# Softmax sums in another accumulator bank, a regrouped plan and new instruction orders in a one-core two-layer decode kernel

## The chip, the cores and the metric

The kernel runs on one core of a Trainium2 chip. A core has a matrix engine (TensorE, PE in the profile), a vector engine (VectorE, DVE), a scalar engine (ScalarE, ACT), a general engine (GpSimd, POOL) and one that here only issues transfers (SyncE, SP). Each engine runs its own list of instructions in the order in which they are written; engines wait for one another, and for transfers, by semaphores. Matrix products are accumulated in eight PSUM banks. The metric is the device time in microseconds (us) of one launch; smaller is better.

## The reference

One decode step for four tokens (one position each), width D = 448, through attention and a gated FFN, twice with the same weights and the same caches:

```python
x = A_x                                          # [4, 1, 448] bf16
x = x + attn(layernorm(x), k_cache, v_cache, wq, wo)
x = x + ffn(layernorm(x), w_gate, w_up, w_down)   # (silu(x@wg) * (x@wu)) @ wd, inner width 1792
x = x + attn(layernorm(x), k_cache, v_cache, wq, wo)
x = x + ffn(layernorm(x), w_gate, w_up, w_down)
```

`attn` has 16 query heads of 256, two to each of 8 key/value heads, and looks at the last 2048 of the 8192 cached positions: scores = q·k / 16, softmax, times v, then the output projection `wo`. Each token has keys and values of its own. "Layer 0" and "layer 1" are the two passes; since a token attends only to its cache, one token's layer 1 can run while another is still in layer 0.

## The kernel before, in words

**Store and loads.** One token's K for one key/value head is 1 MB, V another. They are loaded in halves of 512 KB into `half`, a store of 38 units of that size: 31 are free from the start, the last 7 hold `wq` first and are used for K and V only after the last q projection. Of each token's eight heads in layer 0, the six processed last are kept in the store until layer 1 has used them ("kept pairs"); heads 0 and 1 are loaded again. That makes 80 K units and 80 V units; K comes in at L976/L978 (a load of both halves at once where the order says `a+b`) and V at L992, all issued by SP in the order `SEQ_SP` and into the units listed in `SLOTS`. A load into a used unit waits for the instruction that last read it: the scores for K, P times V for V.

**Batches and plan.** `PLAN` is a list of steps; a step has one or more batches, and a batch is two pairs written as token, layer, head: `212+213` is token 2, layer 1, heads 2 and 3. There are 32 batches. The function `group` (from L957) builds one:
- VectorE transposes each newly loaded K unit (L982); GpSimd or VectorE spreads the query `qe` (L1023).
- TensorE makes the scores (L1016) in bank S0 or S1, the two taking turns by batch. VectorE takes the maximum (L1031), TensorE spreads it (L1036, L1039), VectorE negates it (L1045), and ScalarE takes the exponential into `praw` (L1049).
- TensorE turns the probabilities into one of three Y banks (L1060), ScalarE copies them to `pT` (L1068), TensorE sums them (`total`, L1076) and VectorE reduces the sums to `rs` (L1081).
- TensorE multiplies by V into columns 256 to 511 of that Y bank (L1090, four groups of matmuls). GpSimd takes the reciprocal of `rs` (L1103), ScalarE and VectorE copy the product out as `oh` (L1105, L1107), TensorE flips it (L1113), and VectorE scales it into `oT` (L1123).

`out_proj` then multiplies `oT` with `wo_sb` as a column (L1135) or as rows (L1143) into bank A.

**A token's way between its layers.** When all eight heads of a token are through, `rows` (L883 to L897) and `residual` (L903, L875) add up x. `norm` (L589 to L625) takes mean and variance, `ffn` makes gate and up (L801), the activation, and down (L853, the last product of the FFN), a second `norm` follows, and `qproj` (L683 to L722) makes the queries of layer 1 for that token. Banks Z and Z2 serve all of this. Only then can the token's layer 1 begin: its first batch is the scores of kept pairs, which then give their units back.

**What sets the order.** Everything is a node of `Graph`, with the keys it reads and writes and its `bank`. Two instructions on different engines that name the same bank wait for each other in program order, whatever columns they touch. The order on each engine is written out by hand as numbers of nodes: `SEQ_PE`, `SEQ_DVE`, `SEQ_ACT`, `SEQ_POOL`, `SEQ_SP`. A `w` in `SEQ_PE` is a filler (L1253), a matmul of zeros into bank A that keeps TensorE busy; `HELD` says after which filler the readers of bank A may come. `schedule` puts the waits in place.

Of the kernel before, what the change touches and what calls it, by code (L numbers as in the profile page):

```python
# [86 lines left out]
).split()  # L87
SEQ_DVE = (
# [280 lines left out]
def build(nc, A_x, A_k_cache, A_v_cache, A_wq, A_wo, B_x, B_w_gate, B_w_up, B_w_down, out):  # L369
    s0 = A_k_cache.shape[2] - WIN  # L370
    g = Graph()
# [958 lines left out]
```

## Time and profile before

| | |
|---|---|
| median of 3 runs | 283.61 us (282.2 to 283.75) |
| the profiled execution, in all | 285.95 us |
| its span, first to last instruction | 284.2 us |
| mean granted TensorE clock in it | 0.976 |
| TensorE busy, 4437 matmuls | 75% of the span |
| VectorE busy | 61% |
| GpSimd busy | 27% |
| ScalarE busy | 17% |
| moved by DMA | 96.70 MB, 340 GB/s on average |
| of that through the data queues | 96.06 MB, of which 80 MiB are K and V |

The page gives busy shares over the whole span, 40 slices of it, the chain of waits that ended last and the costliest groups of instructions. A group's row reads: line, engine, operation, output and input, shape, count, then busy time and mean ns of one, then the engine's idle time just before such instructions and what ended most of it. A row in the chain, or in a timeline, reads: start in us, length in us, engine, operands, line. A row of the windows reads: stretch, its length, the busy us of PE, weight loads, DVE, ACT and POOL with their counts, the mean granted clock, the DMA share and GB/s. The slices of the DMA's share, in tenths, show where transfers run dry:

```profile
PE   0000077799787888898998598899987889898997
PEclk9999999999779999999999999999998999999998
DMA  6999999999998999998798999937999999499200
```

The first seventh of the span is the loading of weights and first keys, the last tenth has no transfers left.

### The profile page before, as it was taken

Reading aid. Unit: us, or ns where it says so; the run is one execution under the profiler, and the core shown is the slowest. Engines: PE = TensorE matmul, PEld = TensorE weight load, DVE = VectorE, ACT = ScalarE, POOL = GpSimd, SP = SyncE. Lnnn points to the kernel's source line nnn. Section 1 sums busy time; section 2 is a strip of 40 time slices with the busy share of each in tenths; the row PEclk is TensorE's granted clock in tenths of the full one; section 3 lists DMA queues with packets and bytes.
Section 4 is the critical chain, followed back from the end, with each engine's and each line's share of the span. In section 5 each row is a group of like instructions: output and inputs, shape, how many; then the busy total and the mean of one; then the engine's idle time right before and its main releaser. Section 6 shows DMA issues by size and latency. Waiting matters only on the chain.

```text
span 284.2 us, 9987 instructions
## 1 busy us (share of the span) xinstructions
PE 213.9 (75%) x4437; PEld 124.3 (44%) x4437; DVE 174.7 (61%) x522; ACT 47.7 (17%) x115; POOL 76.3 (27%) x195
## 2 busy tenths in 40 slices
PE   0000077799787888898998598899987889898997
PEld 0000032355553533545654253475533545545584
DVE  7716255546434798656568686474997566548751
ACT  0000000232010221221112032201221132023410
POOL 1000027242203322231152035123231331243371
PEclk9999999999779999999999999999998999999998
DMA  6999999999998999998798999937999999499200
GB/s 238 405 413 409 408 413 406 405 404 396 380 386 309 329 407 412 407 409 340 243 343 310 413 411 409 404 148 300 381 379 413 409 408 371 164 338 406 78 5 3
DMA packets 28330, 96.70 MB, mean 340 GB/s; under 512 B 2811, under 2 KB 6911, under 8 KB 27519
## 3 DMA queue, kind: packets, MB, share of 16 engines
q1 hardware_dynamic: 28279, 96.06, 87.4%
q8 instruction: 35, 0.57, 0.8%
q14 instruction: 8, 0.07, 0.1%
q10 hardware_dynamic: 8, 0.00, 0.0%
HBM read 96.05 MB, written 0.00 MB: 338 GB/s over the span
## 4 chain that ended last, share of the span: by engine, by line
PE 46%; DMA 30%; SPq 9%; DVE 6%; issue 3%; ACT 3%; POOL 2%; ACTq 0%
DMA half<-in_A_k_cache_dram 13%; PE A L1253 12%; PE S L1016 8%; DMA wd_sb<-in_B_w_down_dram 6%; DMA half<-in_A_v_cache_dram 6%; DMA wo_sb<-in_A_x_dram 6%; PE Y L1090 5%; SPq L976 4%; PE Z L801 4%; SPq L992 3%; PE Z L683 3%; PE Z L853 3%; DVE half L982 3%; PE A L1143 2%; PE Y L1060 2%
## 5 line engine op out<-in xcount | busy, mean ns | idle before, releaser
L982 DVE STREAM_TRANSPOSE half<-half 128x1024 uint32<-128x1024 uint32 x80 | 97.4, 1230 | 23.9 <-DMA half<-in_A_k_cache_dram 23.8
L1253 PE MATMUL A<-identb,small 128*128 128x512 bf16 x236 | 72.6, 403 | 1.1 <-ACT wide L883 0.8
L1103 POOL TENSOR_TENSOR small<-small 128x4 f32<-128x4 f32 x32 | 32.5, 1018 | 52.3 <-DVE small L1081 49.0
L1090 PE MATMUL Y<-half,pT 128*8 128x256 bf16 x1024 | 38.8, 273 | 3.2 <-DVE small L1081 1.7
L1016 PE MATMUL S<-half,qe 128*8 128x256 bf16 (+1 forms) x1120 | 36.0, 272 | 6.6 <-DVE half L982 4.0
L1016 PEld LDWEIGHTS S<-half,qe 128*8 128x8 bf16 x1120 | 24.6, 85 | 17.1 <-DVE half L982 5.9
L921 PE MATMUL Z<-identb,wo_sb 4*128 4x4 bf16 x4 | 0.3, 166 | 37.6 <-DMA wo_sb<-in_A_x_dram 37.6
L1023 POOL TENSOR_TENSOR qe<-qc,small 128x64 bf16<-128x64 bf16 x56 | 15.4, 295 | 47.6 <-PE S L1016 36.9
L1253 PEld LDWEIGHTS A<-identb,small 128*128 128x128 bf16 x236 | 20.0, 105 | 16.7 <-issue 8.6
L1090 PEld LDWEIGHTS Y<-half,pT 128*8 128x8 bf16 x1024 | 21.1, 85 | 12.0 <-DVE small L1081 4.2
L615 POOL TENSOR_SCALAR st<-st 128x1 f32<-128x1 f32 x16 | 4.5, 283 | 80.4 <-DVE st L609 80.3
L1031 DVE TENSOR_REDUCE small<-S 104x1 bf16<-104x256 f32 x32 | 13.3, 416 | 18.7 <-PE S L1016 18.7
L1105 ACT ACTIVATE oh<-Y 128x256 bf16<-128x256 f32 x32 | 12.2, 383 | 55.2 <-PE Y L1090 46.7
L1107 DVE SCALAR_TENSOR_TENSOR oh<-oh,small,Y 128x256 bf16<-128x256 bf16 x32 | 14.9, 467 | 4.0 <-ACT oh L1105 3.8
L921 PEld LDWEIGHTS Z<-identb,wo_sb 4*128 4x128 bf16 x4 | 0.2, 102 | 37.6 <-DMA wo_sb<-in_A_x_dram 37.6
L1068 ACT ACTIVATE pT<-Y 128x192 bf16<-128x192 f32 x32 | 10.5, 329 | 23.3 <-PE Y L1060 16.7
L1143 PE MATMUL A<-wo_sb,oT 128*4 128x448 bf16 x200 | 14.0, 352 | 0.4 <-DVE oT L1123 0.4
L683 PE MATMUL Z<-half,small 128*5 128x512 bf16 x160 | 11.8, 379 | 2.9 <-DVE small L592 1.5
L1049 ACT ACTIVATE praw<-S,small,st 104x256 bf16<-104x256 f32 x16 | 9.0, 563 | 26.8 <-DVE small L1045 24.9
L1049 ACT ACTIVATE praw<-S,small 104x256 bf16<-104x256 f32 x16 | 7.6, 472 | 32.0 <-DVE small L1045 31.2
L1060 PE MATMUL Y<-selt,praw 104*64 104x48 bf16 x256 | 9.9, 194 | 3.6 <-ACT praw L1049 3.6
L1123 DVE TENSOR_TENSOR oT<-Y,small 128x4 bf16<-128x4 f32 x64 | 8.4, 156 | 5.8 <-PE Y L1113 4.5
(135 smaller groups left out, 244.2 us busy)
## 6 DMA issues: line engine op xcount, KB each, us to landing
half<-in_A_v_cache_dram SPq DMA_DIRECT2D x80, 512.0 KB, 12.7
half<-in_A_k_cache_dram SPq DMA_DIRECT2D x74, 512.0 KB, 8.6
wo_sb<-in_A_wo_dram SPq DMA_DIRECT2D x8, 448.0 KB, 13.2
half<-in_A_wq_dram SPq DMA_DIRECT2D x3, 1024.0 KB, 14.3
half<-in_A_k_cache_dram SPq DMA_DIRECT2D x3, 1024.0 KB, 15.3
wd_sb<-in_B_w_down_dram SPq DMA_DIRECT2D x1, 1568.0 KB, 17.2
wg_sb<-in_B_w_gate_dram SPq DMA_DIRECT2D x1, 1344.0 KB, 10.7
wu_sb<-in_B_w_up_dram SPq DMA_DIRECT2D x1, 1344.0 KB, 15.2
```

The source lines that it names most:

```text
L683: last = e.matmul(zb[32 * j:32 * j + B + 1, 0:512], lhsT=lhsT, rhs=wq_sb[:, c:c + 512], start=(cc == 0), stop=(cc == 3), skip_group_check= ...
L982: return e.transpose(a, a)
L1016: last = e.matmul(Sb[s_][qd:qd + 8, c0:c0 + rhs.free_size()], lhsT=qe[q_][:, P, ce, :, :].rearrange("p a n -> p (a n)"), rhs=rhs, start=(c ...
L1023: g.op(*((DVE, 0.13) if layer and fresh.get(t, gi) == gi else (POOL, 0.25)), pos - SLEAD - 1, lambda e, P=P, t=t, kvh=kvh: e.tensor_tensor ...
L1031: g.op(DVE, (0.23, 0.36)[n - 1], pos, lambda e: e.tensor_reduce(pmax[s_][0:R, :], Sb[s_][0:R, 0:N], AX.X, ALU.max), r=(f"s{s_}",), w=(f"pm ...
L1049: return e.activation(praw[0:R, 0:128 * n].rearrange("p (g r l) -> p g r l", g=2 * n, l=2), Sb[s_][0:R, 0:128 * n].rearrange("p (l g r) -> ...
L1060: last = e.matmul(Yb[p_][64 * h:64 * h + 64, c0:c0 + (48 if n == 2 else 32)], lhsT=praw[0:R, 64 * gg:64 * gg + 64], rhs=w, start=(gg == 0) ...
L1090: last = e.matmul(Yb[p_][32 * gg:32 * gg + M, 256:512], lhsT=pT[pt][:, gg, 2 * a + hv, 4 * P:4 * P + M] if n == 2 else p1[:, gg % 2, 2 * a ...
L1103: g.op(POOL, 0.69, pos, lambda e: e.tensor_tensor(ri[p_][:, 0:2 * n], rs[p_][:, 0:2 * n], expo[:, 1:1 + 2 * n], op=ALU.pow), r=(f"rs{p_}", ...
L1107: g.op(DVE, 0.43, pos, lambda e: e.scalar_tensor_tensor(out=oh[:, :], in0=oh[:, :], scalar=lomask[:, 0:1], in1=Yb[p_][:, 256:512], op0=ALU ...
L1143: last = e.matmul(Ab[32 * k:32 * k + B, 0:D], lhsT=oT[oi][:, k % 2, k // 2, :], rhs=wo_sb[:, 4 * kvh + k, :], start=False, stop=False, ski ...
L1253: return e.matmul(Ab[:, 0:512], lhsT=zero[:, 0:1].broadcast_to([128, 128]), rhs=identb[:, :].unsqueeze(1).broadcast_to([128, 4, 128]), sta ...
```

## The change

Three things, in one diff.

**1. The sums.** The sum over the probabilities is written to columns 288 and up of the batch's score bank, where it went to columns 192 and up of its Y bank. The reduction reads it there. The first of the two matmuls now starts its accumulation, since the bank isn't zeroed ahead. The node names the S bank for both, so P times V no longer waits for the reduction by way of the Y bank, and the scores of the batch that takes the same S bank next do.

```diff
-            sums = Yb[p_][:, 192:192 + 32 * n].rearrange("p (k P n) -> p k P n", k=16, n=2)
+            sums = Sb[s_][:, 288:288 + 32 * n].rearrange("p (k P n) -> p k P n", k=16, n=2)
 
             def total(e):
...
-                                    start=False, stop=False, skip_group_check=True)
+                                    start=(P == 0), stop=False, skip_group_check=True)
                 return last
-            g.op(PE, 0.06 * n, pos, total, r=(f"pT{pt}", "onesb"), w=(f"ysum{p_}",), bank=(f"Y{p_}",))
+            g.op(PE, 0.06 * n, pos, total, r=(f"pT{pt}", "onesb"), w=(f"m{s_}",), bank=(f"S{s_}",))
             g.op(DVE, 0.2, pos, lambda e: e.tensor_reduce(
                 rs[p_][:, 0:2 * n].rearrange("p (P n) -> p P n", n=2), sums.rearrange("p k P n -> p P n k"), AX.X, ALU.add),
-                r=(f"ysum{p_}",), w=(f"rs{p_}",), bank=(f"Y{p_}",))
+                r=(f"m{s_}",), w=(f"rs{p_}",), bank=(f"S{s_}",))
```

**2. The plan.** Two steps of token 1's kept pairs become one, and token 2's kept pairs are put together otherwise:

```diff
-    "106+107", "200+201", "010+011", "115+113", "116+112", "114+117", "202+203", "204+205", "206+207", "300+301",
-    "212+213 214+215", "216+217 302+303", "306+305", "304+307", "110+111", "210+211 316+313", "314+315",
+    "106+107", "200+201", "010+011", "115+113", "116+112 114+117", "202+203", "204+205", "206+207", "300+301",
+    "212+213 217+215", "216+214 302+303", "306+305", "304+307", "110+111", "210+211 316+313", "314+315",
     "312+317", "310+311",
```

**3. The orders.** `SEQ_PE`, `SEQ_DVE`, `SEQ_ACT`, `SEQ_POOL`, `SEQ_SP`, `SLOTS` and `HELD` are new lists throughout. Apart from the fillers (232 for 236), the instructions on each compute engine are the same in number and kind. SP has 175 issues for 176, since four K loads are paired for three. Compared instruction by instruction, with batches named by token, layer and head:

- VectorE, beginning of token 1's stage: maximum and negation of 100+101 come ahead of the last steps of token 0's FFN (L835 to L846).
- VectorE, end of token 1's and token 2's last batches: the transposition of a K unit of 010 comes ahead of the scaling of 107's output, that of one of 301 ahead of 207's; before, behind them. At the maximum of 316+313, two transpositions of 311 stand ahead; before, one of 310.
- TensorE: scores 100+101 lie inside token 0's gate and up; sum and first P times V of 100+101 lie ahead of token 0's q projection. P times V of 010+011 and of 200+201 lie ahead of the scores of 112 and 113; before, the first behind both. P times V of 300+301 lies between the parts of token 2's q projection, and token 2's down projection stands behind scores 300+301, two fillers and the spread of their maximum. P times V of 313 and 315 lies ahead of the scores of 317.
- TensorE's fillers up to the down projection of tokens 0, 1, 2 and 3: 53, 119, 171 and 217, for 48, 115, 162 and 221 before.
- SP: the last V load of token 2's layer 0 is at place 117 for 119, with 66.69 MB in front of it for 67.21. Five loads, for six, use the space of `wq`. Each load is directed to another unit.

```diff
 SLOTS = (
-    "0 1 2 3 4 5 6 7 8 9 10 11 12 13 14 15 16 17 18 19 20 21 22 23 24 25 26 27 28 29 30 14 15 18 19 26 4 28 8 9 10 18 "
...
+    "0 1 2 3 4 5 6 7 8 9 10 11 12 13 14 15 16 17 18 19 20 21 22 23 24 25 26 27 28 29 30 9 10 15 23 24 18 30 17 11 21 "
...
```

More of the change, by code (lines that the diff above doesn't have):

```diff
@@ L125 @@
 SEQ_SP = (
[7 rows of a table removed]
[7 rows of a table added]
 ).split()
 SLOTS = (
[4 rows of a table removed]
[4 rows of a table added]
 ).split()
 HELD = (
-    "0 44 44 44 102 102 108 108 140 142 142 142 151 151 158 158 208 208 215 215 227 228 228 228 228 228 228 228 228 "
-    "228 228 228"
+    "0 44 44 46 106 106 116 116 136 142 145 145 159 159 166 166 213 213 213 213 218 220 224 224 224 224 224 224 224 "
+    "224 224 224"
 ).split()
```

128 rows, old and new, of tables (SEQ_ACT, SEQ_DVE, SEQ_PE, SEQ_POOL) are left out of this document.

## The prediction

> **What bounds the kernel now.** I read the page first, for the busy shares:
>
> ```profile
> PE 213.9 (75%) x4437; PEld 124.3 (44%) x4437; DVE 174.7 (61%) x522; ACT 47.7 (17%) x115; POOL 76.3 (27%) x195
> ```
>
> No engine is full. Then the windows, cut at the ends of the four tokens' first layers (columns: stretch, length, busy us of PE, PEld, DVE, ACT, POOL, then the granted PE clock, the DMA share and GB/s):
>
> ```profile
> 84.40:127.00 42.60, 37.27 (x687) 19.38 (x685) 29.51 (x68) 8.62 (x22) 12.75 (x29) 1.00 0.98 379
> 127.00:149.00 22.00, 20.47 (x484) 13.19 (x483) 13.47 (x47) 3.35 (x8) 6.46 (x18) 1.00 0.85 312
> 149.00:184.00 35.00, 27.47 (x562) 14.34 (x561) 24.01 (x59) 7.93 (x20) 10.47 (x23) 1.00 1.00 389
> 184.00:203.00 19.00, 18.02 (x460) 12.09 (x459) 12.13 (x41) 2.44 (x6) 5.53 (x17) 1.00 0.69 266
> 203.00:238.00 35.00, 29.93 (x538) 15.31 (x537) 24.89 (x54) 8.58 (x21) 9.86 (x21) 0.95 1.02 399
> 238.00:258.00 20.00, 18.62 (x443) 11.73 (x444) 12.53 (x42) 2.04 (x5) 5.47 (x16) 1.00 0.79 283
> 258.00:284.20 26.20, 22.27 (x595) 15.97 (x587) 14.75 (x68) 7.03 (x17) 9.89 (x24) 0.93 0.26 100
> ```
>
> Loads and a chain take turns. In the long stretches the transfers are full (0.98 to 1.02). In the stretches where a token passes from attention through its FFN to its next q, they run dry: 22.0 x 0.15 = 3.3 us, 19.0 x 0.31 = 5.9 us, 20.0 x 0.21 = 4.2 us are lost. There all 31 units of the K/V store are taken, and a load is issued only when the scores or P times V of a batch give a unit back. SyncE's own timeline shows the largest hole:
>
> ```profile
> 174.43 18.47 SPq L992 DMA_DIRECT2D half<-in_A_v_cache_dram  x3
> 192.94 2.02 SPq L976 DMA_DIRECT2D half<-in_A_k_cache_dram  x2
> ```
>
> Three issues take 18.47 us: the second of them waits for the scores of 300+301, which end at 192.06. So the path is: a token's last loads land, chain to the next scores, units given back, loads, the next token. After the last loads a chain of 26 us remains. The chain of waits has the stage ends on which I count (start, us, what):
>
> ```profile
> 83.39 1.05 PE Z L853 x42
> ...
> 92.95 2.09 PE S L1016 x56
> ...
> 138.98 1.50 PE Z L853 x56
> ...
> 182.43 0.17 PE Y L1076 x2
> ...
> 182.62 0.23 DVE small L1081
> ...
> 182.90 1.05 PE Y L1090 x32
> ...
> 192.06 1.50 PE Z L853 x56
> ...
> 248.24 1.50 PE Z L853 x56
> ```
>
> L853 is the FFN's down projection: tokens 0 to 3 are through it at 84.44, 140.48, 193.56 and 249.74. The span is 284.2.
>
> **The change part by part.** *Sums into the scores' bank.* Nothing is added or removed: the same two matmuls, the same reduction, at the prices of these rows:
>
> ```profile
> L982 DVE STREAM_TRANSPOSE half<-half 128x1024 uint32<-128x1024 uint32 x80 | 97.4, 1230 | 23.9 <-DMA half<-in_A_k_cache_dram 23.8
> ...
> L1031 DVE TENSOR_REDUCE small<-S 104x1 bf16<-104x256 f32 x32 | 13.3, 416 | 18.7 <-PE S L1016 18.7
> ...
> L1081 DVE TENSOR_REDUCE small<-Y 128x4 f32<-128x64 f32 x32 | 6.8, 213 | 5.7 <-PE Y L1076 5.2
> ```
>
> What moves is a wait. Now P times V cannot begin before the reduction has read the bank that both use; the source view of L1090 lists it as its largest releaser:
>
> ```profile
> its engine sat idle before it (us, times) until:
>   DVE small L1081: 5.9, 16
> ```
>
> In the order as built, 26 P times V waited for that reduction; in the new one none does, and 8 scores do (batches 005, 017, 107, 117, 203, 214, 307, 317 by token, layer, head), because there are two score banks and a batch reuses the bank of the batch before last. Removed: at most 5.9 us, on the path only where the chain goes through it. Added: from 0 (the reduction ran earlier) to one transposition and the reduction itself, 1.23 + 0.21 = 1.44 us each, 11.5 us for eight, since VectorE takes its instructions in order and some reductions now stand behind a transposition that waits for a K load. I take 0 for most, because other work of TensorE stands between sum and scores, and count the one in the tail below. The Trainium skill's PSUM — Partial Sum Buffer, section "PSUM bank collisions raise a hardware error", says that two engines must be kept apart by bank and quadrant and not by address; so separate columns would not excuse the new wait any more than the old. The rule speaks against giving the scarcer bank (two against three) the longer use, and by it alone the sum would be +11.5 - 5.9 = +5.6 us; the row of 5.9 us bears out the wait, not its new place.
>
> *Plan and orders.* The counts stay (1120 score matmuls, 80 transpositions, 96 MB), with 232 fillers for 236. So only places matter. I walked the new order stage by stage with the durations above, a stage ending with L853; each price below is bounded by 0 and the row that it names.
>
> Token 0, to 84.44: the maximum of 100+101 (0.42 by the row of L1031) and its smaller negation come ahead of the FFN's last VectorE steps, which had been done by then: **+0.5**.
>
> Token 1, 84.44 to 140.48. The q projection now has the sum and the first P times V of 100+101 ahead of it rather than the waiting P times V inside it; before, TensorE also stood still inside it with no releaser:
>
> ```profile
> 88.85 0.59 PE L683 MATMUL Z<-half,small 128*5 128x512 bf16 x5 [1.22 <-issue]
> ```
>
> The first kept scores ended about 9.6 us after the FFN (92.95 plus half of 2.09); I get 8.1: -1.5, of which 1.22 is that stop. P times V of 100+101 also frees four units earlier, so the loads that follow need not pause; but VectorE (29.5 of 42.6 us busy, transpositions waiting their turn) does not pass that on. At the end of the stage the order of these two rows turns round:
>
> ```profile
> 130.01 0.23 DVE L1123 TENSOR_TENSOR oT<-Y,small 128x4 bf16<-128x4 f32 x2
> 130.16 1.23 DVE L982 STREAM_TRANSPOSE half<-half 128x1024 uint32<-128x1024 uint32 x1
> ```
>
> The transposition stands first: +1.2 on the chain, seven fillers covering it on TensorE. Another transposition leaves the norm's steps, where about 0.8 of its 1.23 was not covered: -0.8; some 0.4 is left. Sum **-1.1**.
>
> Token 2, 140.48 to 193.56. Its last V load is two places further forward in the queue, 0.52 MB at the 399 GB/s of the full stretch from 203: -1.3. P times V of 010+011 and 200+201 come ahead of the scores of 112 and 113, units come back several us earlier and the queue does not empty: up to -3.3 by the first window; VectorE passes on -2.2 in my walk. The last P times V no longer stands behind sum, reduction and two semaphores (182.43 to 182.90) and an output projection: -1.1. Against that, again a transposition goes ahead of the scaled output (+1.2), and the down projection stands behind scores, two fillers and the maximum's spread (+0.8). Sum **-2.6**.
>
> Token 3, 193.56 to 249.74. P times V of 300+301 comes into the q projection, between its parts: loads start 1.5 to 2 us earlier after the hole of 5.9: -1.7. The last P times V began here,
>
> ```profile
> 236.41 1.05 PE L1090 MATMUL Y<-half,pT 128*8 128x256 bf16 x32
> ```
>
> behind the scores of 111 and their spread; now it goes ahead of 111's later steps, one score batch (32 matmuls, about 1.1 us) fewer: -1.1. Sum **-2.8**. If the landing alone set both, -5.9 - 4.2; if VectorE alone, 0.
>
> Tail. Before the maximum of 313 two transpositions stand instead of one (+1.2); P times V of 313 and 315 moves ahead of the scores of 317 (-0.4), whose wait for its reduction stands behind two transpositions. **+0.8**. Five loads instead of six wait for the last q projection; the data is there in both orders, so nothing is counted; were it not, one load is 1.3 us.
>
> Total 0.5 - 1.1 - 2.6 - 2.8 + 0.8 = -5.2 us. My walk has no stop without a releaser, and the trace has: the 1.22 above, and smaller ones; I put back 2.0, an estimate. **-3.2 us.** The profiled execution took 285.95 in all for its span of 284.2, and the median of the runs is 283.61, 2.3 below; I take the difference from the median: 280.4, forecast **280.5 us**.
>
> **The rivals.** *Slower, by VectorE's queue.* The reduction that frees a score bank is late by the transposition ahead of it, and that one by its load. For it: 23.8 us of VectorE's idle time end with a K load (the row of L982), and the new order has it so for 203, 307 and 317. Against: TensorE has fillers there. It decides from the point where the reduction runs more than 1.2 us after its sum. Price 3 x 1.44 = 4.3 with the other gains not passed on: 283.6 + 4.3 = 287.9 us.
>
> *Nothing comes of it.* Units come back earlier, loads land earlier, and the K tiles wait for VectorE instead; the two transpositions put ahead of the outputs eat the rest. For it: 24.9 of 35.0 us busy in the fifth window. About 283.5 us.
>
> *All of it arrives.* If VectorE never binds, two thirds of the 13.4 us of holes go: 283.6 - 8.9 = 274.7 us. Against: the transpositions are in the order, and they do not shrink.
>
> *The clock.* Token 3's stage has 46 fillers for 59. The half-speed stretch behind a pause is in the trace:
>
> ```profile
> 216.40 0.20 PE L1113 MATMUL Y<-small,oh 128*128 128x4 bf16 x2 [1.97 <-DVE oh L1107]
> 216.47 1.95 PE L1253 MATMUL A<-identb,small 128*128 128x512 bf16 x7
> ...
> 218.31 2.29 PE L1253 MATMUL A<-identb,small 128*128 128x512 bf16 x5
> ```
>
> A pause of 1.97 us, then 279 ns a filler, then 458. Three more stretches like it (2.3 us, 40% of it lost) cost 2.8 and, with the gains of tokens 2 and 3 gone, the time is 283.6 + 0.5 - 1.1 + 0.8 + 2.8 = 286.6 us. The Trainium skill's TensorE: Matmul & The Clock Gate, Part 1, lets the clock fall after an idle window of about 3.4 us; by that rule a gap this short would cost nothing and the forecast would stand; the trace shows the drop behind 1.97 us.
>
> **How the numbers follow.** Forecast 0.43, nothing 0.14, all 0.14, VectorE's queue 0.24, clock 0.05. A measurement of this kernel tells 0.5% (1.4 us) from no change. Faster: 0.40 of the forecast, 0.14 and 0.01: 0.55. Slower: 0.24, 0.03 and 0.03: 0.30. Same: 0.15. The forecast's own range is 277.3 (nothing put back, and the 3.3 in full: 283.6 - 5.2 - 1.1) to 283.3 (two more waits of 1.44 on the path). The whole range reaches both outer cases, 274.5 to 289.0: below, 274.7; above, 287.9 and a little of the 11.5 us bound.
>
> **What would show it.** No P times V released by L1081, and L1016 released by it for under 2 us: the moved wait costs nothing; over 4 us: the slower rival. DMA share in the stretch behind token 2's FFN above 0.69 and the second stretch above 0.85: the freed units. The down projections ending near 84.9, 139.9, 190.4 and 243.8, plus up to 2 us: the stages. A transposition directly ahead of the pair of scaled outputs of 107 and 207, and TensorE waiting there: the +1.2. The forecast is wrong if token 2's down projection ends after 194, or if the tail after token 3's is over 36.5 us.

## The result, and the profile after

The changed kernel takes 279.02 us (median of 6 runs, 278.38 to 281.44); the kernel before, with the runs made beside it, 282.9 (6 runs, 281.26 to 285.86). The ratio is 0.9866, interval 0.982 to 0.9912: faster by 3.9 us where the forecast had 3.1 (283.6 to 280.5). Here and below a time is the median of all runs, while a ratio and its interval leave out the slow runs of each kernel, so a ratio is not the quotient of the two medians beside it. The profiled execution of the changed kernel took 279.4 for a span of 277.6. The page's busy shares of the changed kernel have moved by a point or two:

```profile
PE 212.1 (76%) x4433; PEld 125.9 (45%) x4433; DVE 173.7 (63%) x522; ACT 47.2 (17%) x115; POOL 76.2 (27%) x195
```

The instructions are the same in number but for four fillers, and TensorE is busy 1.8 us less, VectorE 1.0, so the gain is in the main waiting time. The windows of the changed kernel, cut near the same places of each token's way as those of before (columns as there), the last row with another cut for token 2:

```profile
83.20:124.80 41.60, 35.77 (x667) 19.36 (x666) 28.83 (x68) 7.78 (x20) 11.63 (x28) 1.00 1.02 395
124.80:146.50 21.70, 20.59 (x489) 13.30 (x491) 12.57 (x45) 3.94 (x10) 7.13 (x17) 1.00 0.84 311
146.50:181.00 34.50, 30.37 (x624) 16.59 (x613) 25.78 (x67) 8.10 (x21) 10.93 (x27) 1.00 1.01 397
181.00:198.50 17.50, 16.60 (x430) 11.67 (x428) 11.57 (x40) 2.06 (x5) 5.96 (x19) 1.00 0.75 282
198.50:232.00 33.50, 27.54 (x526) 14.24 (x527) 23.38 (x51) 8.65 (x21) 9.07 (x17) 1.00 1.03 407
232.00:251.00 19.00, 16.07 (x439) 11.37 (x435) 12.80 (x42) 2.58 (x6) 5.90 (x18) 1.00 0.91 350
251.00:277.60 26.60, 23.79 (x592) 16.96 (x588) 14.73 (x69) 6.40 (x16) 9.88 (x23) 0.87 0.19 72
...
177.90:198.50 20.60, 18.84 (x466) 13.08 (x467) 14.53 (x45) 2.44 (x7) 6.21 (x20) 1.00 0.79 301
```

The full stretches are as full as they were. Of the dry ones, that behind token 1 stays as it was (0.84 for 0.85), and that behind token 3 went from 0.79 to 0.91 and is shorter (19.0 for 20.0). For token 2 the row from 181.00 begins 3.1 us behind the last P times V, where that of before begins right at it. Cut there too, as in the last row, the stretch has 0.79 for 0.69 and is longer (20.6 for 19.0). By the forecast's measure the three lose 3.5, 4.3 and 1.7 us, for 3.3, 5.9 and 4.2. The chain of waits of the changed kernel has these down projections (start, us, what):

```profile
136.25 0.80 PE Z L853 x28
137.14 0.70 PE Z L853 x28
...
187.59 1.56 PE Z L853 x56
...
240.68 1.15 PE Z L853 x42
...
242.37 0.52 PE Z L853 x14
```

Tokens 1 to 3 are through at 137.84, 189.15 and 242.89, for 140.48, 193.56 and 249.74; token 0 at 83.23 for 84.44. The source view of P times V (L1090) no longer names the reduction:

```profile
its engine sat idle before it (us, times) until:
  DMA half<-in_A_v_cache_dram: 5.0, 7
  ACT pT L1068: 2.2, 5
  issue: 2.2, 7
```

and that of the scores (L1016) names it for next to nothing:

```profile
  DVE small L1081: 0.8, 2
```

The same view of the kernel before has the same 0.8 us, so on the scores nothing was added that the profile shows.

The source view adds up two rows of the page, weight loads (PEld) and matmuls (PE), and one wait can stand in both. In the page of the kernel before, the 5.9 us of P times V are these:

```profile
L1090 PE MATMUL Y<-half,pT 128*8 128x256 bf16 x1024 | 38.8, 273 | 3.2 <-DVE small L1081 1.7
...
L1090 PEld LDWEIGHTS Y<-half,pT 128*8 128x8 bf16 x1024 | 21.1, 85 | 12.0 <-DVE small L1081 4.2
```

The matmuls themselves stood still for 1.7 us behind the reduction.

SyncE's largest hole is still there, with four issues in 18.20 us for three in 18.47, but it ends at 187.57 instead of 192.94:

```profile
169.33 18.20 SPq L992 DMA_DIRECT2D half<-in_A_v_cache_dram  x4
187.57 5.57 SPq L976 DMA_DIRECT2D half<-in_A_k_cache_dram  x4
```

### The profile page after: what moved, and what is told of

Same layout as the page of the kernel before. It is cut to its first block, busy times and chain, and to the rows that moved or that the text cites. A ratio compares the mean times of both kernels' runs of the same rounds, so it can differ in the third digit from the quotient of the medians.

```text
span 277.6 us, 9978 instructions
## 1 busy us (share of the span) xinstructions
PE 212.1 (76%) x4433; PEld 125.9 (45%) x4433; DVE 173.7 (63%) x522; ACT 47.2 (17%) x115; POOL 76.2 (27%) x195
## 4 chain that ended last, share of the span: by engine, by line
PE 47%; DMA 30%; SPq 9%; DVE 8%; ACT 2%; issue 2%; ACTq 0%
DMA half<-in_A_v_cache_dram 14%; PE A L1253 12%; DMA half<-in_A_k_cache_dram 11%; PE Y L1090 9%; PE S L1016 6%; SPq L992 5%; DMA wo_sb<-in_A_x_dram 5%; PE Z L683 4%; DVE half L982 3%; PE Z L801 3%; PE Z L853 2%; SPq L558 2%; PE Y L1060 2%; PE A L1135 2%; PE A L1143 2%
## 5 line engine op out<-in xcount | busy, mean ns | idle before, releaser
L1253 PE MATMUL A<-identb,small 128*128 128x512 bf16 x232 | 67.8, 393 | 0.7 <-ACT wide L883 0.4
L1103 POOL TENSOR_TENSOR small<-small 128x4 f32<-128x4 f32 x32 | 32.4, 1015 | 82.1 <-DVE small L1081 72.7
L1090 PE MATMUL Y<-half,pT 128*8 128x256 bf16 x1024 | 40.2, 273 | 2.8 <-DMA half<-in_A_v_cache_dram 2.2
L1016 PE MATMUL S<-half,qe 128*8 128x256 bf16 (+1 forms) x1120 | 35.2, 269 | 4.1 <-DVE wide L835 1.1
L1016 PEld LDWEIGHTS S<-half,qe 128*8 128x8 bf16 x1120 | 25.2, 85 | 12.4 <-DVE half L982 2.7
L1090 PEld LDWEIGHTS Y<-half,pT 128*8 128x8 bf16 x1024 | 19.7, 85 | 10.3 <-DMA half<-in_A_v_cache_dram 2.8
L1143 PE MATMUL A<-wo_sb,oT 128*4 128x448 bf16 x200 | 14.6, 352 | 2.9 <-DVE oT L1123 2.8
L1081 DVE TENSOR_REDUCE small<-S 128x4 f32<-128x64 f32 x32 | 6.8, 211 | 8.3 <-PE S L1076 8.1
```

What stands on the lines that cost most here:

```text
L1016: last = e.matmul(Sb[s_][qd:qd + 8, c0:c0 + rhs.free_size()], lhsT=qe[q_][:, P, ce, :, :].rearrange("p a n -> p (a n)"), rhs=rhs, start=(c ...
L1090: last = e.matmul(Yb[p_][32 * gg:32 * gg + M, 256:512], lhsT=pT[pt][:, gg, 2 * a + hv, 4 * P:4 * P + M] if n == 2 else p1[:, gg % 2, 2 * a ...
L1103: g.op(POOL, 0.69, pos, lambda e: e.tensor_tensor(ri[p_][:, 0:2 * n], rs[p_][:, 0:2 * n], expo[:, 1:1 + 2 * n], op=ALU.pow), r=(f"rs{p_}", ...
L1143: last = e.matmul(Ab[32 * k:32 * k + B, 0:D], lhsT=oT[oi][:, k % 2, k // 2, :], rhs=wo_sb[:, 4 * kvh + k, :], start=False, stop=False, ski ...
L1253: return e.matmul(Ab[:, 0:512], lhsT=zero[:, 0:1].broadcast_to([128, 128]), rhs=identb[:, :].unsqueeze(1).broadcast_to([128, 4, 128]), sta ...
```

## The experiments

Edits of the orders are shown with the names of the instructions instead of their numbers: SC scores, PV P times V, T a transposition of K, oT a scaled output, w a filler, each with token, layer and head where it has them. Ratios are to the kernel before, run beside them on the same chip; its medians there were 284.4 to 285.3. Three chips were used and the changed kernel was run again on one of them only, so other versions are compared with it by its two ratios, 0.9866 and 0.9835. "FFN" is the time from a token's last P times V to the end of its down projection.

### The kernel before and the changed one, once more

No edit. 

> The kernel before, unchanged, for a second profile. Its first profile took 285.95 us against a median of 282.9, and its span is 6.6 us longer than that of the changed kernel, where the medians differ by 3.9. Theory A (most of the surplus of 2.7 us is chance of one execution): the down projections of tokens 0 to 3 end 1 to 3 us earlier than 84.44, 140.48, 193.55 and 249.74, and the transfer of wd lands nearer to the 81.47 of the changed kernel than to 82.66. Theory B (the stages are steady and the surplus lies outside the span): they come within 0.3 us of the first profile.

> The changed kernel, unchanged, beside the runs below on one chip and for a second profile. Its ratio to the kernel before was 0.987 (0.982 to 0.991): 0.982 to 0.991 again if that holds on another chip. Its down projections ended at 83.23, 137.84, 189.15 and 242.89; two profiles of the kernel before differ by up to 2 us in token 0 and by 1.4 us in token 3's stage, so the same spread is expected here, and what lies above it in the comparison of stages is the change.

The changed kernel again: 280.37 us, ratio 0.9835 (0.9783 to 0.9887), so the gain holds in a second set of runs. The stages in two profiles of each (us, from the ends of L853; the tail runs to the span's end):

| | token 0 | token 1 | token 2 | token 3 | tail | span | execution |
|---|---|---|---|---|---|---|---|
| before | 84.44 | 56.03 | 53.07 | 56.19 | 34.46 | 284.2 | 285.95 |
| before, again | 86.40 | 55.20 | 53.70 | 54.81 | 35.28 | 285.4 | 287.18 |
| changed | 83.23 | 54.61 | 51.31 | 53.74 | 34.71 | 277.6 | 279.4 |
| changed, again | 83.77 | 53.69 | 53.41 | 53.98 | 34.34 | 279.2 | 281.1 |

Both theories fell: the second profile of before ends its stages later, not earlier, and both profiled executions of before lie 2 to 3 us above their medians (282.9 and 285.04), those of the changed kernel 0.4 and 0.7. So the spans overstate the gain (6.6 and 6.2 us, by the runs 3.9 and 4.7, which is 1.65% of 285.33), and one stage of one profile is good to some 2 us. The first two stages are shorter in both pairs; tokens 2 and 3 by 1.8 and 2.4 in the first pair, 0.3 and 0.8 in the second, in which TensorE's granted clock was 0.50 from 169.1 to 172.5, from 210.0 to 216.9 and from 237.3 to 240.8. The clock favours the first pair: in tokens 1 to 3 the changed kernel has no half speed in its first profile and 13.7 us of it in its second, the kernel before 3.4 and 6.8.

### Sums back in the Y bank

```diff
-            sums = Sb[s_][:, 288:288 + 32 * n]...
+            sums = Yb[p_][:, 192:192 + 32 * n]...
-  PV305 PV305 PV305 sum305 PV305        (and 10 more, TensorE)
+  sum305 PV305 PV305 PV305 PV305
-  oT205 oT205 rs207                     (and 3 more, VectorE)
+  rs207 oT205 oT205
```

> The changed kernel with its orders and its plan, but the sums in the Y bank as before; 11 of the 32 sums and 4 reductions have to come ahead of their P times V. The forecast counted the moved wait at nothing and the release of P times V at 1.1 us in token 2 only: it expects 279.0 + 1 to 2 us. Rival 1, the new bank is the main part of the gain: 282 to 283 us, with L1090 waiting some 5 us for L1081 as before. Rival 2, the bank is worth nothing and the orders are all: 278.7 to 279.3 us, L1090's waits for L1081 under 1 us.

297.03 us, ratio 1.04 (1.0344 to 1.0456): far outside all three. P times V in the page of this kernel:

```profile
L1090 PE MATMUL Y<-half,pT 128*8 128x256 bf16 x1024 | 44.1, 299 | 19.0 <-DVE small L1081 19.0
...
L1090 PEld LDWEIGHTS Y<-half,pT 128*8 128x8 bf16 x1024 | 21.5, 90 | 28.3 <-DVE small L1081 22.0
```

(Its profiled execution had a granted clock of 0.927 and took 304.66, so its stages are not read.) The matmuls stand still for 19.0 us behind the reduction, where they stood for 1.7 in the kernel before and for none in the changed one. In 9.1 of the 19.0 us the reduction came right behind a transposition, in most of the rest behind another of VectorE's steps. Such places cost nothing while P times V does not wait for the reduction. Once it does, the kernel takes some 16 us more than the changed one (297.03 - 0.985 x 285.04).

### Sums in the score bank, orders as before

```diff
-            sums = Yb[p_][:, 192:192 + 32 * n]...
+            sums = Sb[s_][:, 288:288 + 32 * n]...
-  SC117 tP113 w w w tP112 sum113        (and 6 more, TensorE)
+  tP113 w w w tP112 sum113 SC117
-  max117 rs113                          (and 5 more, VectorE)
+  rs113 max117
```

> The kernel before with the sums in the score bank and nothing else, save what that bank forces: seven scores (005, 017, 117, 203, 217, 307, 317) come behind the sum of the batch before last and six reductions ahead of what waits for them. If the bank is the gain, 280 to 282 us. If the scores are what the bank costs (the forecast's bound of 1.44 us each, 203 alone moves by some 4 us), 283 to 287 us: the orders had to be written anew for the bank to be worth anything.

292.61 us, ratio 1.0267 (1.0206 to 1.0328): slower by 7.6, past the upper end of both. P times V no longer waits for the reduction; the scores do (rows of L1016):

```profile
L1016 PE MATMUL S<-half,qe 128*8 128x256 bf16 (+1 forms) x1120 | 37.6, 279 | 7.9 <-DVE small L1081 5.5
...
L1016 PEld LDWEIGHTS S<-half,qe 128*8 128x8 bf16 x1120 | 25.7, 87 | 18.2 <-DVE small L1081 7.8
```

Neither half of the change is a gain: the bank alone, with the moves that it forces, is +2.7%, plan and orders without the bank, again with forced moves, +4%, all together -1.3%. The Trainium skill's PSUM — Partial Sum Buffer, "PSUM bank collisions raise a hardware error", asks for waits by bank and not by address; the program waits so in both banks, and the 5.5 us of the matmuls show that the wait has moved. The sum that the prediction made by that rule alone, +5.6, was for the new orders; that it is near the 7.6 of the old ones is luck, since 5.5 us were added for its 11.5 and 1.7 removed for its 5.9. What made up the rest of the 7.6 us was not followed.

### Outputs ahead of the transposition, without and with cover

```diff
-  T010 oT107 oT107 T011                 (VectorE; the same for T301, oT207)
+  oT107 oT107 T010 T011
-  flip107 w w w w w w w oC106 oC107 w odd10    (TensorE)
+  flip107 w w oC106 oC107 odd10                (first run: 6 w later in the FFN)
+  flip107 w w oC106 oC107 w w w w w w odd10    (second run)
```

> The changed kernel with the scaled outputs of 107 and 207 ahead of the transposition again, and the fillers that covered it moved behind the first gate and up (three of them left out). The forecast put +1.2 us on the chain for each: it expects 279.0 - 2.4 passed on in part, 277 to 278 us, with the down projections of tokens 1 and 2 ending 1 us earlier after the down projection before them. Rival, VectorE has the same transpositions between the last P times V and the norm in either order, so only their order changes: 278.7 to 279.3 us.

> The scaled outputs of 107 and 207 ahead of the transposition, as in the run before, but with all fillers kept: those that stood ahead of the output projection stand right behind it. In the run before, TensorE stood still for 1.37 us behind 107 and 1.59 us behind 207 and ran at half speed for some 3 us after each, so the test was spoilt. If the forecast's +1.2 us a token is right, it is 1 to 2 us faster than the changed kernel on this chip. If VectorE pays the transpositions in either order, it is the same within 0.3%, and the pauses were the whole loss of the run before (about 3 us).

The first: 283.69 us, ratio 0.9975 (0.994 to 1.0011), 1.3% slower than the changed kernel. TensorE's timeline in it (start, us, instruction, in brackets the idle time before it and its releaser):

```profile
130.29 0.18 PE L589 MATMUL Z<-small,twice 128*128 128x1 bf16 x1 [1.37 <-DVE small L875]
...
132.33 1.89 PE L1253 MATMUL A<-identb,small 128*128 128x512 bf16 x4
```

A pause of 1.37 us, and from 131.2 to 134.6 half speed: four fillers take 1.89 us, where three at full speed take 0.81 (a row of the changed kernel under the last experiment). Token 1's FFN took 14.14 us for 11.30. So this run measured the uncovered pause and the clock. With the fillers kept, the second: 281.52, ratio 0.9867 (0.9811 to 0.9922), no different from the changed kernel. VectorE's timeline in the second run,

```profile
127.15 0.23 DVE L1123 TENSOR_TENSOR oT<-Y,small 128x4 bf16<-128x4 f32 x2 [0.35 <-POOL small L1103]
127.29 2.36 DVE L982 STREAM_TRANSPOSE half<-half 128x1024 uint32<-128x1024 uint32 x2
129.75 0.17 DVE L875 TENSOR_TENSOR small<-xr,A 128x4 bf16<-128x4 f32 x1
```

and in the changed kernel:

```profile
127.81 1.24 DVE L982 STREAM_TRANSPOSE half<-half 128x1024 uint32<-128x1024 uint32 x1
128.96 0.20 DVE L1123 TENSOR_TENSOR oT<-Y,small 128x4 bf16<-128x4 f32 x2
129.08 1.23 DVE L982 STREAM_TRANSPOSE half<-half 128x1024 uint32<-128x1024 uint32 x1
130.46 0.17 DVE L875 TENSOR_TENSOR small<-xr,A 128x4 bf16<-128x4 f32 x1 [0.16 <-PE A L1253]
```

Two transpositions stand between the flip and the residual (L875) in either order; only which instruction goes through first has changed. The stretch from the first of these rows to L875 is 2.60 in the one and 2.65 in the other. From the end of token 1's last P times V to L875 it is 4.31 in the second run and 3.92 in the changed kernel: with the outputs first VectorE stands still for 0.35 us until GpSimd's reciprocal (L1103) is there, and a transposition ahead of them fills that time. So in token 1 the price of 1.2 us is paid for having the transpositions there, not for their order. For token 2 this profile does not tell, since it ran at half speed from 179.4 to 189.7 and its FFN took 14.42 us.

### Token 2's last V load two places later

```diff
-  ... V206 V207 K301 K301 V301          (SP; units unchanged)
+  ... V206 K301 K301 V207 V301
```

> The changed kernel with token 2's last V load put back by the two places that the change had won: two K loads of 301 go ahead of it. The forecast put -1.3 us on these places: the last P times V of 207 ends 1.3 us later or more (two loads are 2.6 us; it ended 0.6 us after the landing), and the kernel takes 1 to 2.5 us more. Rival, the transpositions of 301 come earlier by as much and VectorE gives it back: within 0.4 us.

284.01 us, ratio 0.9935 (0.9893 to 0.9977), 0.7 to 1% (2.0 to 2.9 us) slower than the changed kernel with its 0.9866 and 0.9835. TensorE's timeline in it, and two of its windows, show the price in two parts:

```profile
179.82 0.61 PE L1090 MATMUL Y<-half,pT 128*8 128x256 bf16 x16 [1.84 <-DMA half<-in_A_v_cache_dram]
...
181.51 2.29 PE L1253 MATMUL A<-identb,small 128*128 128x512 bf16 x5
```

```profile
177.35:180.76 3.41, 1.45 (x32) 0.73 (x32) 0.84 (x4) 0.82 (x2) 1.01 (x1) 1.00 1.03 410
180.76:191.00 10.24, 9.30 (x174) 6.12 (x178) 6.12 (x17) 0.10 (x1) 1.64 (x6) 0.50 0.27 106
```

1.84 us of waiting for the load, and then fillers of 458 ns: TensorE stays at half speed until 191.0, and token 2's FFN takes 13.67 us for 11.30. The second part is not the load's alone: the profiles of the run before this one and of that with P times V of 300+301 moved have half speed there too, without the later load (token 2's FFN 14.42 and 13.00 us).

### P times V of 010+011 behind the kept scores again

```diff
-  q10 sum011 PV011 q10 ... tq10 w PV011 PV011 sq10 w w PV201 PV201 SC113 SC112
+  q10 sum011 q10 ... tq10 w sq10 w w PV201 PV201 SC113 SC112 PV011 PV011 PV011
```

> The changed kernel with three of the four groups of P times V of 010+011 put behind the scores of 113 and 112 again. The forecast gave -2.2 us of token 2's stage to the units that come back earlier. It expects the last P times V of 207 some 1.5 to 2.5 us later after the down projection of token 1 (40.0 and 42.2 us in two profiles) and 1 to 2.5 us in all (ratio to before 0.989 to 0.994). Rival, VectorE's transpositions set the stage and the units were early enough: ratio 0.983 to 0.988, as the changed kernel.

283.43 us, ratio 0.9997 (0.9958 to 1.0035): the whole gain is gone, more than the forecast's 2.2. The timeline of all engines in this kernel:

```profile
153.62 1.25 DVE L982 STREAM_TRANSPOSE half<-half 128x1024 uint32<-128x1024 uint32 x1 [5.39 <-DMA half<-in_A_k_cache_dram]
...
154.79 0.19 DVE L1081 TENSOR_REDUCE small<-S 128x4 f32<-128x64 f32 x1
...
155.03 1.58 PEld L1016 LDWEIGHTS S<-half,qe 128*8 128x8 bf16 x47 [4.39 <-DVE small L1081]
155.03 1.89 PE L1016 MATMUL S<-half,qe 128*8 128x128 bf16 x48 [3.90 <-DVE small L1081]
```

The three units come back 2.8 to 7 us later, so the load of K 203 lands at 153.6 (150.2 in the changed kernel). Its transposition waits 5.39 us at the head of VectorE's queue, the reduction of 115+113 stands behind it, the scores of 114+117 need the bank that the reduction has to read, and TensorE stands still for 3.90 us, then runs at half speed to 160.1. This is the rival "by VectorE's queue", which had 1.44 us for one such wait: the price is the lateness of the load ahead, so here it was not bounded by one transposition.

### P times V of 300+301 behind the q projection

```diff
-  nm20 PV301 q20 q20 q20 PV301 tq20 PV301 PV301 tq20 sq20
+  nm20 q20 q20 q20 tq20 tq20 sq20 PV301 PV301 PV301 PV301
```

> The changed kernel with the four groups of P times V of 300+301 behind token 2's q projection instead of between its parts. The forecast gave -1.7 us of token 3's stage to loads that start 1.5 to 2 us earlier. It expects the q projection about 1 us shorter, those loads issued 1.5 to 3 us later, the last P times V of 307 some 1 to 2 us later after token 2's down projection (41.6 to 42.3 us in two profiles) and 0.5 to 1.7 us in all (ratio 0.987 to 0.993). Rival, the shorter q projection and its earlier kept scores give as many units back: ratio 0.983 to 0.988.

281.45 us, ratio 0.9925 (0.9885 to 0.9964), some 2 us slower; its interval overlaps those of the changed kernel, so the size is rough. SyncE's timeline in this kernel:

```profile
189.71 7.58 SPq L976 DMA_DIRECT2D half<-in_A_k_cache_dram  x4
```

The four K loads behind the hole take 7.58 us to be issued, 5.57 in the changed kernel: the forecast's "1.5 to 2 us earlier", undone, is 2.01. Token 3's stage is 55.98 us for 53.74 and 53.98, in an execution (283.44 us) that was the longest of eleven, so the stage is no more than a hint.

### The first loads unpaired

```diff
-  V005 K007+K007 K004 K005+K005 K004 K003+K003 ...      (SP)
+  V005 K007 K007 K004 K005 K005 K004 K003 K003 ...
```

> The changed kernel with three of its four paired K loads, all among the first seven issues, made single again (same units, same order). Token 0 ends 1.2 to 2 us earlier than before in every profile of the changed kernel, where the forecast had +0.5; wd, on which its first down projection waits, lands at 81.2 to 81.5 for 82.7 to 84.6, with the same 31.04 MB ahead of it, and 0.4 to 0.5 MB more have landed by 20 us. If the pairs at the start make that, wd lands at 82 us or later, down of token 0 ends about 1 us later and the kernel takes 0.5 to 1.5 us more (ratio to before 0.987 to 0.992). Rival, the order of the first loads and not their pairing: wd at 81.2 to 81.5 and ratio 0.982 to 0.988 as the changed kernel on two chips.

281.33 us, ratio 0.988 (0.9831 to 0.9929): not told apart from the changed kernel by its time. The trace says more. First window of the changed kernel, of this one, and of the kernel before (columns as above; the last is GB/s):

```profile
0.00:12.00 12.00, 0.00 (x0) 0.00 (x0) 10.41 (x56) 0.00 (x0) 0.81 (x9) 1.00 0.86 337
```

```profile
0.00:12.00 12.00, 0.00 (x0) 0.00 (x0) 10.40 (x56) 0.00 (x0) 0.81 (x9) 1.00 0.85 316
```

```profile
0.00:12.00 12.00, 0.00 (x0) 0.00 (x0) 10.33 (x51) 0.00 (x0) 0.81 (x9) 1.00 0.82 306
```

One profile of each would not be enough for such a difference, but every profile has this window. The ten with these pairs have 334 to 340 GB/s, the three with the loads of before 306, 311 and 322. So the 316 of the one without the pairs lies among those of before: as far as one profile tells, the pairs make the whole of what the rate gained, some 20 GB/s, in 12 us 0.25 MB or 0.6 us at the full rate. wd lands at 81.92 here, at 81.18 to 81.49 in the ten, and at 82.17, 82.66 and 84.62 in the three. Both theories hold half: the pairs make 0.4 to 0.7 us of the landing's gain, and the rest is the order of the first loads or chance.

### Token 1's step split again

```diff
-    "115+113", "116+112 114+117", "202+203",
+    "115+113", "116+112", "114+117", "202+203",
```

> The changed kernel with token 1's step of two batches split in two again, all else in its order (one output projection of head 2 comes forward beside that of head 6). With the step of two batches the output projections of heads 6 and 2 come after the outputs of heads 4 and 7 were written over theirs, so they multiply those; split, each head's own output is projected, as in the kernel before for this pair. By the forecast, which gave the merged step no price, the same within 0.3% (ratio 0.983 to 0.988). Rival, the merged step saves waits of VectorE for the output projections ahead of a transposition (about 0.6 us at 166): ratio 0.987 to 0.990.

279.59 us, ratio 0.985 (0.98 to 0.99): the same. Fewer steps buy no time here, and they are not the same sums. There are two buffers `oT` for the outputs of four heads: in a step of two batches the second batch's outputs are written over those of the first before the first's are projected, so here `wo` of heads 6 and 2 multiplies the outputs of heads 4 and 7, and those of 6 and 2 are left out. The kernel before has four steps of two batches, the changed kernel five. The split step is the one to keep.

### A version with the chain ahead of the transpositions

```diff
-  gu10(up) x4 wf10(up) gu10(gate) x2 wf10(gate) w w w SC011 dn10
+  gu10(gate) x2 wf10(gate) gu10(up) x4 wf10(up) w SC011 dn10
-  gu20 SC301 wf20 wf20 w w w spr301 dn20 x4
+  wf20 gu20 wf20 SC301 dn20 x2 spr301 dn20 x2
-  max301 L835 L846                      (VectorE)
+  L835 L846 max301
-  ... wf30 SC211 dn30 x4                (T210 T210 T211 T211 ahead)
+  ... wf30 w w w dn30 x4 SC211          (T211 behind L846)
```

> A version built on the profile of the changed kernel. Token 1: the gate's products ahead of those of up, so that the tanh (134.61) comes about 0.7 us earlier. Token 2: the closing products of gate and up ahead of the scores of 301, the maximum of 301 behind the last VectorE steps of the FFN, three fillers left out, the spread between the products of down. Token 3: scores 210+211 and one of their four transpositions behind the down projection, three fillers moved. By the rows: down of token 1 ends 0.5 us earlier, of token 2 another 0.65, of token 3 another 2, of which 0.5 is given back to the scores behind it. If stage ends carry through to the end, 2 to 3 us faster than the changed kernel; if the loads behind scores 301 and 211 (issued up to 0.9 us later) or the last loads decide, within 0.5 us of it.

280.83 us, ratio 0.9823 (0.9746 to 0.9901): no better than the changed kernel. TensorE's timeline in this version around token 2's down projection,

```profile
186.88 1.11 PE L1016 MATMUL S<-half,qe 128*8 128x256 bf16 x32
187.92 0.86 PE L853 MATMUL Z<-wide,wd_sb 128*128 128x32 bf16 x28
```

and in the changed kernel:

```profile
185.56 1.13 PE L1016 MATMUL S<-half,qe 128*8 128x256 bf16 x32
...
186.69 0.81 PE L1253 MATMUL A<-identb,small 128*128 128x512 bf16 x3
...
187.59 1.56 PE L853 MATMUL Z<-wide,wd_sb 128*128 128x32 bf16 x56
```

The down projection starts 1.04 us behind the start of the scores instead of 2.03. The three FFNs took 10.87, 10.47 and 10.46 us for 11.30, 11.25 to 11.30 and 11.65 to 12.18: each step did what it was made for. But the tail took 35.72 us, where the changed kernel has 34.34 to 34.71. Scores 210+211, which give units back, end 1.15 us behind token 3's down projection there instead of 2.2 ahead; that this lengthened the tail is argued, not shown. No version tried is told apart from the changed kernel as faster.

## Why the prediction came out right, point by point

**The total.** Forecast -3.1, measured -3.9 and, in the second set of runs, -1.65% (4.7 us). The sum of the walk was -5.2 in the spans, and the spans fell by 6.6 and 6.2, so the walk was short by 1.0 to 1.4. The 2.0 were put back for stops without a releaser. What stands in their place is another thing: the profiled executions of before lie 2 to 3 us above their medians and those of the changed kernel 0.4 and 0.7, where the step from execution to median took a fixed 2.3 for both. So the total is right in part by luck: two errors met.

**The moved wait, counted at 0.** Right for this order: the scores wait for 0.8 us in two places, as before, and no P times V waits. The bounds beside it were wrong. "Removed: at most 5.9 us" adds weight loads and matmuls, and the matmuls' part is 1.7; it was also read off the old order, and giving the wait back to the new one costs the matmuls 19.0 us. "1.44 us each" holds only while the load ahead is on time, and it was 3.90 where it was not. What the forecast called two parts, bank and orders, is one.

**Token 0, +0.5: wrong sign.** Measured -1.2, and -2.6 in the second pair. The step priced two VectorE instructions and had no term for the landing of the weights; 31.04 MB up to and with wd are loaded in both kernels. With the new first loads the first 12 us move 334 to 340 GB/s for 306 to 322, and wd lands 0.7 us or more earlier.

**Token 1, -1.1: measured -1.4 and -1.5.** Up to the last P times V -0.9 for the forecast's -1.5, in the FFN -0.5 for +0.4. The +1.2 for the transposition ahead of the outputs was no price of that order (rows of the run with all fillers kept). The expected row is there, T010 directly ahead of the pair of scaled outputs, but TensorE is covered by its fillers.

**Token 2, -2.6: measured -1.8 and -0.3.** Up to the last P times V -3.5 for -4.6 in the first pair; undoing the V places cost 2.0 to 2.9 us (forecast 1.3) and undoing the freed units about 4 (forecast 2.2), each with a half-speed stretch behind a pause in it. They do not add up to the gain: together they are more than all of it. FFN +1.7 for +2.0: the size was right, one cause not. The +0.8 for the down projection's place was regained in full by moving it (10.47 us for 11.30, with three fillers fewer). For the other, this row of the changed kernel's TensorE timeline has another reason:

```profile
178.72 0.35 PE L893 MATMUL Z<-small,wide 128*128 128x1 bf16 x8 [0.87 <-DVE wide L885]
```

The last P times V now ends before the rows of bank A have been copied out (L883, L885). Before, sum, wait and the whole of P times V stood behind the projection whose rows are copied (182.43 to 183.95) and hid the copy; now half of P times V does. That copy was late next, and the forecast did not say so.

**Token 3, -2.8: measured -2.4 and -0.8.** Up to the last P times V -2.35 in the first pair. Undoing the place of P times V of 300+301 cost about 2 us (forecast 1.7).

**Tail, +0.8: measured +0.25 and -0.9**, inside what two profiles of one kernel differ by.

**The rivals.** "Nothing" and "all" are outside the interval. VectorE's queue is real, but in other orders than the one built (the run with P times V of 010+011 late). The clock is real too: it shaped three of the runs that undid a part, and the changed kernel's second profile has three half-speed stretches in tokens 1 to 3 where each profile of before has one. What they cost the changed kernel is not told apart. The Trainium skill's TensorE: Matmul & The Clock Gate, Part 1, puts the fall behind an idle window of some 3.4 us; pauses of 1.37 and 1.84 us were followed by half speed here, so the measured rows decide. The length agrees (stretches of 3.41 us and its multiples, last section); that the window must be idle throughout does not.

The signs of the freed units came half: the DMA share behind token 2's FFN is above 0.69, the second stretch is not above 0.85.

**What is not settled.** How the 3.9 us divide over the stages: one stage of one profile is good to some 2 us, and the clock differs from one profile to the next. And what made wd land earlier beside the pairing of the first loads.

## What to carry to other kernels

A wait that moves from one pair of engines to another is priced in the order that it will stand in, not in the one where it stood: here the bank alone cost 2.7%, plan and orders alone 4%, and all together gained 1.3%. Behind VectorE's in-order queue a wait cost as much as the late load at its head (3.90 us), so what protected this kernel is that buffers come back early. A source view that adds weight loads and matmuls can count one wait twice: take the matmuls' row for what TensorE lost. And when a filler is moved off a pause, look for half speed behind it before the move itself is judged.

## What the runs showed of the hardware

- Half speed comes in whole windows. In the granted clock of all 14 profiles every stretch at 0.50 that ends within the span is 3.41, 6.83 or 10.24 us long, and within one profile the stretches begin whole multiples of 3.41 us apart (with the V load late 180.76 to 191.00, rows above).
- What goes ahead of it is idle time within such a window rather than one long pause. From token 0's to token 3's down projection, in the 13 profiles other than that of 304.66 us: behind a full-speed window in which TensorE stood still for 1.7 us or more in all, the next was at half speed in 8 of 9 cases; for 1.1 to 1.7 us in 9 of 28; for less in 10 of 532. Nine of these ten lie in token 3's FFN, so idle time is not the whole of it.
- The same instructions do not get the same clock twice: the changed kernel's first profile has no half speed between 80 and 267, its second has 3.41, 6.83 and 3.41 us there, from 169.07, 210.03 and 237.34.
- Three 1 MB loads in place of six of 512 KB at the start, with the same bytes in the same order, went with 334 to 340 GB/s in the first 12 us (ten profiles), for 316 in the one without them.
